# Decode attention with two mixed branches: part of one set's query weights as an indirect DMA to 48 partitions

## The chip, the cores and the metric

One Trainium2 chip, one core of it. The metric is the device time of one execution in microseconds, the median of several runs. Each core has sixteen DMA engines; a load of 128 partitions is spread over all of them, 8 partitions each.

## The reference

One token (`x`, 448 wide) goes through two attention branches with cached keys and values, and the outputs are mixed by a gate. All numbers are 32-bit floats. Branch A has 16 heads with a key and a value cache each; branch B has 16 query heads on 8 caches. Each cache is 8192 x 256.

```python
q = x @ wq                       # 16 heads of 256
scores = q . k * 256 ** -0.5     # over 8192 cached keys
o = softmax(scores) . v
branch = o.reshape(4096) @ wo    # back to 448
g = sigmoid((x * gate_w).sum())
out = g * A(x) + (1 - g) * B(x)
```

The caches are 403 MB of the 432 MB that the kernel reads.

## The kernel before

The work is cut into 8 **sets**. A set is one cache of B (unit 2, which serves two query heads) and two heads of A (units 0 and 1). Each unit has 4 **tiles** of 16 x 128 keys; a tile of keys or values is 128 partitions x 4096 columns. TILES numbers the 96 tiles.

Everything that is read lies in DRAM as one array, `stream`, in the order of use. `plan` writes this order: keys of tile i, values of tile i - 3, a set's query weights (`wq`, 3584 columns) a few tiles ahead of the set, its output weights (`wo`, 3584 columns) some tiles after it. It then cuts the order into **fills** of at most FULL = 15872 columns, 7936 KB. Pieces are cut only at multiples of their ATOM (512 columns for keys, values and `wq`, 448 for `wo`). There are 54 fills, numbered from 0; the last three are cut into smaller loads, so that the end is fed in small steps.

The main loop takes a slot of the ring (3 slots, 15936 columns) for each fill, and SP issues its load (L470). SP waits there until the slot's former fill has been read by all who use it. `piece` then emits the work of each piece:

- `project` (L222) multiplies `x` with `wq`. The weights of a set are 14 pieces of 128 rows: the 448 rows of the weights are KF = 3 blocks of 128 and a rest of 64, for the branches B (`a` = 0) and A (`a` = 1). The rests of both lie together in the last piece, one in partitions 0 to 63 and one in 64 to 127. `xz` holds `x` for each block, in column 0 of 32 columns of zeros. The query comes out in PSUM, rows 0 (B) and 32 (A) of `q`, 512 columns, and goes to SBUF (L226). `spread` turns it into the forms that the scores need.
- `scores` (L257 on PE, L263 to L269 on DVE and ACT) for units 2 and 1, `scores_by_row` (L279, L283 on DVE) for unit 0.
- `attend` (L309 on PE) multiplies probabilities with values.
- `gather`, `combine`, `column`, `project_o`, `emit_set` end a unit and a set; some of them are put off by a number of tiles with `wait`.

The first fill begins with `xg`: 4 columns of `x` and 4 of `gate_w`. `inputs` (L194 to L196) copies `x` into `xz`. Ahead of that, POOL and DVE make constants. POOL does nothing after them. At the end PE multiplies the last set with its output weights (L399), DVE copies 112 columns (L484), SP stores them (L485). The names of the tiles in the profile are `slot` (the ring), `sm` (small PSUM tiles, the query too), `o` (attention output), `Y` (final sum).

Of the kernel before, what the change touches and what calls it, by code (L numbers as in the profile page):

```python
# [7 lines left out]
F32 = mybir.dt.float32  # L8
BF16 = mybir.dt.bfloat16
AF = mybir.ActivationFunctionType  # L10
OP = mybir.AluOpType
# [3 lines left out]
P = 128  # L15
D = 448
DH = 256
SK = 8192
NCOL = SK // P
KF = D // P  # L20
KR = D - KF * P
# [3 lines left out]
NS = 8  # L25
ROWS = 16
NT = NCOL // ROWS
FULL = 15872
LEAD = 3
BLK = 32  # L30
NB = ROWS
# [3 lines left out]
WQ = (4 * KF + 2) * DH  # L35
# [4 lines left out]
TILES = [((s, r), t) for s in range(NS) for r in UNITS for t in range(NT)]  # L40


XG = 2 * (KF + 1)
SLOT = 15936
ATOM = {"xg": XG, "k": 2 * DH, "v": 2 * DH, "wq": 2 * DH, "wo": D}


def plan():

    size = {"xg": XG, "k": ROWS * DH, "v": ROWS * DH, "wq": WQ, "wo": 8 * D}  # L50
    per = len(UNITS) * NT
    n = len(TILES)
    items = []
    for i in range(n + LEAD):
        if i == 0:
            items += [("xg", 0), ("wq", 0)]
        if i < n:
            items.append(("k", i))
        if i >= LEAD:
            items.append(("v", i - LEAD))  # L60
        if i % per == 7 and i // per + 1 < NS:
            items.append(("wq", i // per + 1))
        if i % per == LEAD + 1 and i >= per:
            items.append(("wo", i // per - 1))
    loads, room = [[]], FULL
    last = [("v", n - 3), ("v", n - 2)]
    for kind, i in items[:items.index(last[0])]:
        at, left = 0, size[kind]
        while left:
            step = min(left, room) // ATOM[kind] * ATOM[kind]  # L70
            if step:
                loads[-1].append((kind, i, at, step))
            at, left, room = at + step, left - step, room - step * (kind != "xg")
            if left:
                loads.append([])
                room = FULL

    loads = [[x] for x in loads]
    x = loads[-2][0]
    loads[-2] = [x[:2], x[2:]]  # L80
    loads[-1] += [[(kind, i, 0, size[kind])] for kind, i in last]
    at, end = 0, []
    for c in LAST_CUT:
        end.append([("v", n - 1, at, c * DH)])
        at += c * DH

    for h, e, n in ((3, 0, 2), (0, 0, 2), (1, 0, 3), (2, 1, 1)):
        end.append([("wo", NS - 1, (2 * h + e) * D, n * D)])
    return loads + [end]


LOADS = plan()


@with_exitstack
def kernel(
    ctx: ExitStack,
    tc: tile.TileContext,
    stream: bass.AP,
    out: bass.AP,  # L100
):
    nc = tc.nc
# [5 lines left out]
    const = ctx.enter_context(tc.tile_pool(name="const", bufs=1))  # L108
    small = ctx.enter_context(tc.tile_pool(name="small", bufs=2))
    ps_sc = ctx.enter_context(tc.tile_pool(name="ps_sc", bufs=2, space=PSUM))  # L110
    ps_o = ctx.enter_context(tc.tile_pool(name="ps_o", bufs=3, space=PSUM))
    ps_s = ctx.enter_context(tc.tile_pool(name="ps_s", bufs=2, space=PSUM))
# [69 lines left out]

    xz = const.tile([P, KF + 2, BLK], F32, name="xz")
    nc.vector.memset(xz, 0.0)
    gate = const.tile([1, 2], F32, name="gate")

    def clear(t, n):
# [3 lines left out]
    YY = [ps_y.tile([P, D], F32, name="Y")]  # L191

    def inputs(xs):
        nc.vector.tensor_copy(xz[:, :KF, 0], xs[:, :KF])  # L194
        nc.vector.tensor_copy(xz[:KR, KF, 0:1], xs[:KR, KF:])  # L195
        nc.vector.tensor_copy(xz[KR:, KF + 1, 0:1], xs[KR:, KF:])  # L196

    def prepare(gw):
        clear(YY[0], D)
        gp = ps_s.tile([1, 1], F32, name="sm")  # L200
        for c in range(KF + 1):
            nc.tensor.matmul(gp, xz[:, c, 0:1], gw[:, c:c + 1], start=(c == 0), stop=(c == KF))
        ge = const.tile([1, 1], F32, name="ge")
        nc.scalar.activation(ge, gp, AF.Exp, scale=-1.0)
        nc.vector.tensor_scalar(ge, ge, 1.0, None, op0=OP.add)
        nc.vector.reciprocal(gate[:, 0:1], ge)
        nc.vector.tensor_scalar(gate[:, 1:2], gate[:, 0:1], -1.0, 1.0, op0=OP.mult, op1=OP.add)
# [3 lines left out]
    QR, SC, QA = {}, {}, {}  # L211

    def project(s, c0, w):

        if c0 == 0:
            QR[s] = ps_s.tile([2 * BLK, 2 * DH], F32, name="sm")
        q = QR[s]
        for j in range(w.shape[1]):
            a, c = divmod(c0 + j, KF)
            for a in (a,) if a < 2 else (0, 1):  # L220
                c = c if c0 + j < 2 * KF else KF
                nc.tensor.matmul(q[BLK * a:BLK * (a + 1), :], xz[:, c if c < KF else KF + a, :], w[:, j, :],  # L222
                                 start=(c == 0), stop=(c == KF), skip_group_check=True)
        if c0 + w.shape[1] == 2 * KF + 1:
            QR[s] = small.tile([P, NB * BLK], F32, name="px")[:2 * BLK, :2 * DH]
            nc.scalar.activation(QR[s], q, AF.Copy)  # L226

    def spread(s):

        qt = ps_s.tile([P, 2, 2, 2], F32, name="sm")  # L230
        qr = QR.pop(s)
        for h in range(2):
            for e in range(2):
                at = h * DH + e * P
                nc.tensor.matmul(qt[:, h, e, :], qr[:, at:at + P], rows4[:2 * BLK, :2], start=True, stop=True)
        for r, a, h, M in ((2, 0, 0, 2), (0, 1, 0, 1), (1, 1, 1, 1)):
            if (s, r) in BY_ROW:
                qa = ps_s.tile([P, DH], F32, name="sm")
                nc.tensor.matmul(qa, spread32, qr[:, h * DH:(h + 1) * DH], start=True, stop=True)  # L239
                QA[s, r] = small.tile([P, DH], F32, name="qa", bufs=1)  # L240
                nc.scalar.activation(QA[s, r], qa, AF.Copy, scale=-scale)
                continue
            nc.vector.tensor_scalar(QB[s % 2, r][:, :, BLK:BLK + M], qt[:, h:h + M, :, a].rearrange("p h e -> p e h"),
                                    -scale, None, op0=OP.mult)
# [155 lines left out]
                                 start=False, stop=(last and e == 1), skip_group_check=True)  # L400


    LAST, GW = {}, {}
    per = len(UNITS) * NT
    todo = []

    def wait(n, f, *args):
        todo.append([n, f, args])

    def tick():  # L410
        for t in todo:
            t[0] -= 1
        for t in [t for t in todo if t[0] <= 0]:
            todo.remove(t)
            t[1](*t[2])

    def piece(kind, i, at, view):
        n = view.shape[-1] // ATOM[kind]
        j0 = at // ATOM[kind]
        if kind == "xg":  # L420
            inputs(view[:, :KF + 1])
            GW[0] = view[:, KF + 1:]
        elif kind == "wq":
            project(i, j0, view.rearrange("p (c n) -> p c n", c=n))
            if j0 + n < 2 * KF + 1:
                pass
            elif i == 0:
                spread(0)
                prepare(GW[0])
            else:  # L430
                wait(1, spread, i)
        elif kind == "k":
            u, t = TILES[i]
            if u in BY_ROW:
                scores_by_row(u, t, 2 * j0, view.rearrange("p (j d) -> p j d", d=DH))
            else:
                scores(u, t, j0, view.rearrange("p (c n) -> p c n", c=n))
            if j0 + n < 2 * NG:
                return
            tick()  # L440
            if t == NT - 1:
                gather(u)
                wait(1, combine, u)
                wait(2, column, u)
        elif kind == "v":
            u, t = TILES[i]
            n = view.shape[-1] // DH
            attend(u, t, at // DH, n, view.rearrange("p (j d) -> p j d", d=DH))
            if at // DH + n == ROWS:
                if t == NT - 1:  # L450
                    take(u)
                    if u != TILES[-1][0]:
                        wait(1, project_o, u)
                if i >= len(TILES) - LEAD:
                    tick()
        elif kind == "wo" and i < NS - 1:
            emit_set(i, j0, view.rearrange("p (c n) -> p c n", c=n))
            if i == NS - 2 and j0 + n == 8:
                fold()
        else:  # L460
            for j in range(n):
                LAST[divmod(j0 + j, 2)] = view[:, j * D:(j + 1) * D]

    off = 0
    for fill in LOADS:
        buf = ring.tile([P, SLOT], F32, name="slot")
        c = 0
        for load in fill:
            n = sum(x[3] for x in load)
            nc.sync.dma_start(buf[:, c:c + n], stream[off:off + P * n].rearrange("(p n) -> p n", p=P))  # L470
            off += P * n
            for x in load:
                piece(*x[:3], buf[:, c:c + x[3]])
                c += x[3]
    assert not todo
    s = NS - 1
# [76 lines left out]
```

## Time and profile before

| | |
|---|---|
| median of 3 runs | 1008.62 us (1008.54 to 1008.72) |
| the profiled execution | 1009.04 us |
| its span, first to last instruction | 1007.3 us |
| granted TensorE clock, mean | 0.778 |
| PE, DVE, ACT, POOL busy | 570.1, 458.2, 92.9, 1.9 us |
| DMA | 432.51 MB, mean 429 GB/s |

A row of the table of groups names the line, the engine, the operation, what it writes and reads, how often; then busy time in us, the mean of one in ns, and the idle time of the engine just ahead of it with what ended it. In a table of windows each row has the busy time of PE, weight loads, DVE, ACT and POOL in that stretch with the number of instructions, then the granted clock, the share of time in which the sixteen DMA engines were busy, and GB/s. A row of a DMA queue has packets, megabytes and the time of its packets as a share of sixteen engines' time; a packet counts where it begins, so that in a short window the share can go over 100%. A row of the timeline has start, duration, engine, line, operation and in brackets the idle time ahead of it. A row of DMA issues ends with the time from issue to landing.

### The profile page before, as it was taken

To read this page: it belongs to the slowest core of one execution; us is meant where nothing else is said; L and a number is where in the kernel's file an instruction comes from. 1 tells how busy PE (TensorE), PEld (TensorE's weight loads), DVE (VectorE), ACT (ScalarE), POOL (GpSimd) and SP (SyncE) were. 2 spreads that over 40 slices of the span, in tenths; PEclk is the share of its full clock that TensorE was granted. 3 is DMA by queue.
4 is the path that set the end of the run, shared out by engine and by line. 5 is a ranking of instruction groups with operands and counts; after the bars stand their busy time and mean duration, and the time that the engine had idled before them with its cause. 6 is when DMAs were issued, how large, how long until landed. Compare 5 with 4: busy or idle time off the path is not lost.

```text
span 1007.3 us, 7568 instructions
## 1 busy us (share of the span) xinstructions
PE 570.1 (57%) x3154; PEld 167.1 (17%) x3154; DVE 458.2 (45%) x644; ACT 92.9 (9%) x307; POOL 1.9 (0%) x10
## 2 busy tenths in 40 slices
PE   0845835664655555646646465545565647536557
PEld 0211211121111111112111121111111112101112
DVE  1386313961248521576215841248521585216851
ACT  0100100010100110001100001100110100101010
POOL 0000000000000000000000000000000000000000
PEclk9977877778786787787777777776787867777788
DMA  9999999999999999999999999999999999999997
GB/s 404 440 439 411 442 439 437 421 437 436 439 424 436 429 439 431 437 429 440 429 434 434 436 429 429 441 437 424 430 442 439 429 424 437 439 441 429 424 422 315
DMA packets 9114, 432.51 MB, mean 429 GB/s; under 512 B 1016, under 2 KB 1144, under 8 KB 1784
## 3 DMA queue, kind: packets, MB, share of 16 engines
q1 hardware_dynamic: 9080, 432.02, 99.2%
q8 instruction: 25, 0.41, 0.1%
q14 instruction: 9, 0.07, 0.0%
HBM read 432.02 MB, written 0.00 MB: 429 GB/s over the span
## 4 chain that ended last, share of the span: by engine, by line
DMA 72%; DVE 15%; PE 11%; ACT 1%; issue 1%; another core or an unknown queue 0%; SPq 0%; ACTq 0%; DVEq 0%
DMA slot<-in_stream_dram 72%; DVE sr L283 6%; DVE slot L279 6%; PE o L309 5%; PE sc L257 4%; PE sm L222 1%; ACT px L266 0%; DVE mn L263 0%; DVE pr L296 0%; ACT pxr L292 0%; DVE pr L269 0%; ACT ew L348 0%; DVE wr L355 0%; PE sm L373 0%
## 5 line engine op out<-in xcount | busy, mean ns | idle before, releaser
L309 PE MATMUL o<-slot,pr 128*32 128x512 f32 (+1 forms) x1536 | 342.3, 740 | 224.0 <-DMA slot<-in_stream_dram 223.9
L257 PE MATMUL sc<-slot,qb 128*32 128x512 f32 x1024 | 195.2, 713 | 112.1 <-DMA slot<-in_stream_dram 111.9
L263 DVE TENSOR_REDUCE mn<-sc 128x1 f32<-128x512 f32 x64 | 44.1, 690 | 332.5 <-PE sc L257 314.2
L279 DVE TENSOR_TENSOR slot<-slot,qa 128x4096 f32<-128x4096 f32 (+7 forms) x40 | 142.6, 3565 | 42.7 <-DMA slot<-in_stream_dram 42.7
L309 PEld LDWEIGHTS o<-slot,pr 128*32 128x32 f32 (+1 forms) x1536 | 78.6, 139 | 402.9 <-DMA slot<-in_stream_dram 253.7
L283 DVE TENSOR_REDUCE sr<-slot 128x16 f32<-128x4096 f32 (+7 forms) x40 | 142.7, 3567 | 1.4
L257 PEld LDWEIGHTS sc<-slot,qb 128*32 128x32 f32 x1024 | 45.9, 129 | 226.0 <-issue 120.0
L266 ACT ACTIVATE px<-sc,st 128x512 f32<-128x512 f32 x64 | 44.0, 688 | 407.0 <-DVE st L264 395.1
L269 DVE STREAM_TRANSPOSE pr<-px 128x512 f32<-128x512 f32 x64 | 45.6, 713 | 59.6 <-ACT px L266 59.6
L222 PE MATMUL sm<-slot,xz 128*32 128x512 f32 x128 | 45.9, 695 | 37.6 <-DVE xz L195 22.8
L292 ACT ACTIVATE pxr<-sr,st 128x16 f32<-128x16 f32 x32 | 9.8, 308 | 373.0 <-DVE st L290 373.0
L373 PE MATMUL sm<-sel,ob 128*128 128x1 f32 (+1 forms) x96 | 16.7, 278 | 35.8 <-DVE ob L319 35.8
L319 DVE SCALAR_TENSOR_TENSOR ob<-o,half,ob 128x256 f32<-128x256 f32 x24 | 11.3, 473 | 45.1 <-ACT ob L318 45.0
L373 PEld LDWEIGHTS sm<-sel,ob 128*128 128x128 f32 x96 | 14.7, 217 | 59.7 <-DVE ob L319 52.1
L222 PEld LDWEIGHTS sm<-slot,xz 128*32 128x32 f32 x128 | 11.1, 126 | 66.7 <-issue 27.2
L296 DVE TENSOR_TENSOR pr<-pxr,cols 128x256 f32<-128x256 f32 x32 | 13.6, 426 | 15.9 <-ACT pxr L292 15.9
L318 ACT ACTIVATE ob<-o,half 128x256 f32<-128x256 f32 x24 | 11.3, 470 | 42.7 <-PE o L309 42.7
L362 PE MATMUL sm<-ones,wr 1*128 1x1 f32 x48 | 9.5, 265 | 9.1 <-DVE wr L355 9.1
L239 PE MATMUL sm<-px,spread 64*128 64x256 f32 x16 | 6.6, 497 | 14.1 <-DVE es L349 14.1
L382 PE MATMUL Y<-slot,ocs 128*1 128x448 f32 x112 | 14.4, 633 | 0.0
L362 PEld LDWEIGHTS sm<-ones,wr 1*128 1x128 f32 x48 | 7.7, 200 | 31.8 <-issue 29.9
L266 ACT ACTIVATION_READ_ACCUMULATOR px<-sc,st 128x1 f32 x64 | 12.3, 193 | 0.0
(73 smaller groups left out, 138.4 us busy)
## 6 DMA issues: line engine op xcount, KB each, us to landing
slot<-in_stream_dram SPq DMA_DIRECT2D x50, 7936.0 KB, 42.4
slot<-in_stream_dram SPq DMA_DIRECT2D x1, 7940.0 KB, 21.8
slot<-in_stream_dram SPq DMA_DIRECT2D x1, 4864.0 KB, 41.2
slot<-in_stream_dram SPq DMA_DIRECT2D x2, 2048.0 KB, 25.2
slot<-in_stream_dram SPq DMA_DIRECT2D x1, 3072.0 KB, 30.0
slot<-in_stream_dram SPq DMA_DIRECT2D x1, 1280.0 KB, 20.7
slot<-in_stream_dram SPq DMA_DIRECT2D x1, 1024.0 KB, 24.3
slot<-in_stream_dram SPq DMA_DIRECT2D x2, 512.0 KB, 25.5
```

What stands on the lines that cost most here:

```text
L222: nc.tensor.matmul(q[BLK * a:BLK * (a + 1), :], xz[:, c if c < KF else KF + a, :], w[:, j, :], start=(c == 0), stop=(c == KF), skip_group_ ...
L257: nc.tensor.matmul(sc[32 * g:32 * (g + 1), :], qb[:, e, at:at + 32], kt[:, j, :], start=(e == 0), stop=(e == 1), skip_group_check=True)
L263: nc.vector.tensor_reduce(mn, sc, axis=AX.X, op=OP.min)
L266: nc.scalar.activation(px, sc, AF.Exp, bias=st[:, 0, t:t + 1], scale=-1.0, accum_out=st[:, 1, t:t + 1])
L269: nc.vector.transpose(pr.rearrange("p (q r k) -> p q k r", r=BLK, k=2), px.rearrange("p (q k c) -> p q k c", c=BLK, k=2))
L279: nc.vector.tensor_tensor(kt, kt, QA[u][:, None, :].to_broadcast([P, n, DH]), op=OP.mult)
L283: nc.vector.tensor_reduce(sc[:, j0:j0 + n], kt, axis=AX.X, op=OP.add)
L296: nc.vector.tensor_tensor(pr, px[:, :, None, :].to_broadcast([P, ROWS // 2, NG * NT, 2]), cols[:, t].rearrange("p g r -> p (g r)")[:, None ...
L309: nc.tensor.matmul(O[u][w * g:w * (g + 1), :], pr[:, j // 2, :w], vt[:, j - j0:j - j0 + 2, :], start=(t == 0 and j < 2 * P // w), stop=(t ...
L362: nc.tensor.matmul(cl, WR.pop(u).rearrange("p c x m k -> p (c x m k)"), ones[:1, :], start=True, stop=True)
L373: nc.tensor.matmul(oc[:, e, :M], OB[u][:, e::2], SEL[u][:, :M], start=True, stop=True)
L382: nc.tensor.matmul(YY[0][32 * h:32 * h + 1, :], OC[s, r][:, e, m:m + 1], wt[:, j, :], start=False, stop=(s == NS - 2 and e == 1), skip_gro ...
```

## The change

Set 4's query weights of branch B, 3 blocks of 128 rows with 512 columns, are cut at column SW = 416. The first 416 columns leave the stream. They go, 384 rows in all, to a second array `side` of 128 x 3328: SIDE_ROWS names 48 partitions, each holds 8 whole rows of 416 columns, the other 80 hold zeros. The 48 partitions are those for which 8 * (p >> 6) + (p >> 2) % 8 is one of 0, 2, 4, 7, 8, 15. In `at`, each of these partitions has its own number, each other one its number plus 100000, which is out of bounds.

At fill 23 the slot's first 3328 columns are set aside for `side`, and POOL loads them with one indirect DMA, whose rows out of bounds are skipped. The fill's part of the stream has 12064 columns in place of 15872. All that comes later is cut at other places; the number of fills stays 54. The stream has 842544 columns in place of 843784.

The set's other weights (`ws`, 2336 columns: 3 blocks of 96 columns of B, 3 blocks of 512 of A, the rests) come as one piece, not cut. `project_side` takes the place of `project` for this set: 2 products of the rests, 3 of A's blocks, 3 with 96 columns, and 8 that multiply a column of `x8` with 416 columns of `side`. `x8` holds `x` in the layout of the 48 partitions; it comes in 8 more columns of `xg`. `at` is made at the start by two iotas on POOL and seven small operations on DVE.

```diff
+SIDE_SET = 4
+SIDE_FILL = 23
+SIDE_ENGINES = (0, 2, 4, 7, 8, 15)
+SIDE_ROWS = [p for p in range(P) if (8 * (p >> 6) + (p >> 2) % 8) in SIDE_ENGINES]
+SC8 = KF * P // len(SIDE_ROWS)
+SW = 416
+SREST = 2 * DH - SW
+SIDE = SC8 * SW
+XG = 2 * (KF + 1) + SC8
...
-            items.append(("wq", i // per + 1))
+            items.append(("ws" if i // per + 1 == SIDE_SET else "wq", i // per + 1))
...
-                room = FULL
+                room = FULL - SIDE * (len(loads) - 1 == SIDE_FILL)
...
     def inputs(xs):
+        nc.vector.tensor_copy(x8, xs[:, 2 * (KF + 1):])
...
+    def project_side(s, view, far):
+
+        q = ps_s.tile([2 * BLK, 2 * DH], F32, name="sm")
+        near = view[:, :KF * SREST].rearrange("p (c n) -> p c n", c=KF)
+        full = view[:, KF * SREST:].rearrange("p (c n) -> p c n", c=KF + 1)
+        for a in range(2):
+            nc.tensor.matmul(q[BLK * a:BLK * (a + 1), :], xz[:, KF + a, :], full[:, KF, :], start=True, stop=False,
+                             skip_group_check=True)
+        for c in range(KF):
+            nc.tensor.matmul(q[BLK:2 * BLK, :], xz[:, c, :], full[:, c, :], start=False, stop=(c == KF - 1),
+                             skip_group_check=True)
+            nc.tensor.matmul(q[:BLK, SW:], xz[:, c, :], near[:, c, :], start=False, stop=(c == KF - 1),
+                             skip_group_check=True)
+        for c in range(SC8):
+            nc.tensor.matmul(q[0:1, :SW], x8[:, c:c + 1], far[:, c * SW:(c + 1) * SW], start=False, stop=(c == SC8 - 1),
+                             skip_group_check=True)
+        copy_out(s, q)
...
-    for fill in LOADS:
+    for f, fill in enumerate(LOADS):
         buf = ring.tile([P, SLOT], F32, name="slot")
         c = 0
+        if f == SIDE_FILL:
+            c = SIDE
+            FAR[0] = buf[:, :c]
+            nc.gpsimd.indirect_dma_start(FAR[0], None, side, bass.IndirectOffsetOnAxis(at[:, :1], 0),
+                                         bounds_check=P - 1, oob_is_err=False)
```

On PE, at fill 23, behind the products of tile 40's values, this stood before (the line numbers are those of the kernel before; `sm` is the query, `sc` the scores of tile 44):

```order
L309 MATMUL o<-slot,pr 32x512 [waits DMAHW7_49]
L309 MATMUL o<-slot,pr 32x512 x7
L222 MATMUL sm<-slot,xz 32x512 x8
L257 MATMUL sc<-slot,qb_133 32x512 x8
L341 MATMUL sm<-gs_1604,ones 1x32 [waits DVE_49,Activation_49]
```

and this now, with the line numbers of the changed kernel (L351 is `attend`, L299 `scores`):

```order
L351 MATMUL o<-slot,pr 32x512 [waits DMAHW7_49]
L351 MATMUL o<-slot,pr 32x512 x7
L258 MATMUL sm<-slot,xz 32x512 x2
L261 MATMUL sm<-slot,xz 32x512
L263 MATMUL sm<-slot,xz 32x96
L266 MATMUL sm<-slot,x_139 1x416 [waits DMASW0_49]
L266 MATMUL sm<-slot,x_139 1x416 x7
L299 MATMUL sc<-slot,qb_133 32x512 x3
L299 MATMUL sc<-slot,qb_133 32x512 [waits DMAHW0_49]
```

(the rows of L261 and L263 come three times in turn). The eight products became sixteen, the ninth waits for the indirect DMA, and the scores of tile 44 now wait for fill 24 in the middle, since that tile's keys are cut there.

On POOL, which had nothing behind its constants, these rows end its program now:

```order
L170 IOTA px 128x128 [waits DVE_49]
L196 IOTA at 128x1
L197 IOTA at 128x1
L516 DMA slot<-in_side_dram,at 128x3328 [waits DMAHW2_49,DMAHW3_49,DMAHW1_49,DMAHW4_49,DMAHW0_49,DMAHW5_49,DVE_49,DMAHW6_49,PE_49,Pool_49]
L614 UNCONDITIONAL_BRANCH
```

The DMA waits for the former fills of this slot and for their readers; SP's load of the rest of fill 23 does not stand behind it.

More of the change, by code (lines that the diff above doesn't have):

```diff
@@ L40 @@
 TILES = [((s, r), t) for s in range(NS) for r in UNITS for t in range(NT)]
-XG = 2 * (KF + 1)
+SIDE_SET = 4
[7 more added lines that the diff above has]
+XG = 2 * (KF + 1) + SC8
 SLOT = 15936
-ATOM = {"xg": XG, "k": 2 * DH, "v": 2 * DH, "wq": 2 * DH, "wo": D}
+ATOM = {"xg": XG, "k": 2 * DH, "v": 2 * DH, "wq": 2 * DH, "wo": D, "ws": KF * SREST + (KF + 1) * 2 * DH}
 def plan():
-    size = {"xg": XG, "k": ROWS * DH, "v": ROWS * DH, "wq": WQ, "wo": 8 * D}
+    size = {"xg": XG, "k": ROWS * DH, "v": ROWS * DH, "wq": WQ, "wo": 8 * D, "ws": ATOM["ws"]}
     per = len(UNITS) * NT
@@ L99 @@
     stream: bass.AP,
+    side: bass.AP,
     out: bass.AP,
@@ L184 @@
     nc.vector.memset(xz, 0.0)
+    x8 = const.tile([P, SC8], F32, name="x8")
+    at = const.tile([P, 4], mybir.dt.int32, name="at")
+    nc.gpsimd.iota(at[:, 0:1], pattern=[[0, 1]], base=0, channel_multiplier=1)
+    nc.gpsimd.iota(at[:, 1:2], pattern=[[0, 1]], base=sum(1 << e for e in SIDE_ENGINES), channel_multiplier=0)
+    nc.vector.tensor_scalar(at[:, 2:3], at[:, 0:1], 3, 8, op0=OP.logical_shift_right, op1=OP.bitwise_and)
+    nc.vector.tensor_scalar(at[:, 3:4], at[:, 0:1], 2, 7, op0=OP.logical_shift_right, op1=OP.bitwise_and)
+    nc.vector.tensor_tensor(at[:, 2:3], at[:, 2:3], at[:, 3:4], op=OP.bitwise_or)
+    nc.vector.tensor_tensor(at[:, 1:2], at[:, 1:2], at[:, 2:3], op=OP.logical_shift_right)
+    nc.vector.tensor_scalar(at[:, 1:2], at[:, 1:2], 1, 1, op0=OP.bitwise_and, op1=OP.bitwise_xor)
+    nc.vector.tensor_scalar(at[:, 1:2], at[:, 1:2], 100000.0, None, op0=OP.mult)
+    nc.vector.tensor_tensor(at[:, 0:1], at[:, 0:1], at[:, 1:2], op=OP.add)
     gate = const.tile([1, 2], F32, name="gate")
@@ L193, in inputs @@
     def inputs(xs):
+        nc.vector.tensor_copy(x8, xs[:, 2 * (KF + 1):])
         nc.vector.tensor_copy(xz[:, :KF, 0], xs[:, :KF])
-        nc.vector.tensor_copy(xz[:KR, KF, 0:1], xs[:KR, KF:])
-        nc.vector.tensor_copy(xz[KR:, KF + 1, 0:1], xs[KR:, KF:])
+        nc.vector.tensor_copy(xz[:KR, KF, 0:1], xs[:KR, KF:KF + 1])
+        nc.vector.tensor_copy(xz[KR:, KF + 1, 0:1], xs[KR:, KF:KF + 1])
     def prepare(gw):
@@ L224, in project, with copy_out @@
         if c0 + w.shape[1] == 2 * KF + 1:
-            QR[s] = small.tile([P, NB * BLK], F32, name="px")[:2 * BLK, :2 * DH]
-            nc.scalar.activation(QR[s], q, AF.Copy)
+            copy_out(s, q)
+    def copy_out(s, q):
+        QR[s] = small.tile([P, NB * BLK], F32, name="px")[:2 * BLK, :2 * DH]
+        nc.scalar.activation(QR[s], q, AF.Copy)
+    def project_side(s, view, far):
[13 more added lines that the diff above has]
+                             skip_group_check=True)
+        copy_out(s, q)
     def spread(s):
@@ L400, in emit @@
                                  start=False, stop=(last and e == 1), skip_group_check=True)
-    LAST, GW = {}, {}
+    LAST, GW, FAR = {}, {}, {}
     per = len(UNITS) * NT
@@ L420, in piece @@
         if kind == "xg":
-            inputs(view[:, :KF + 1])
-            GW[0] = view[:, KF + 1:]
+            inputs(view)
+            GW[0] = view[:, KF + 1:2 * (KF + 1)]
+        elif kind == "ws":
+            project_side(i, view, FAR[0])
+            wait(1, spread, i)
         elif kind == "wq":
@@ L502, in wq, with apart, rows8 @@
         return _np.concatenate(full + [_np.concatenate(rest, axis=1)[:, :, None]], axis=2).reshape(NS, P, WQ)
+    def apart(w):
+        w = w.reshape(D, NS, 2 * DH)[:, SIDE_SET]
+        rest = w[:KF * P, SW:].reshape(KF, P, SREST).transpose(1, 0, 2).reshape(P, KF * SREST)
+        far = _np.zeros((P, SIDE), w.dtype)
+        far[SIDE_ROWS] = w[:KF * P, :SW].reshape(len(SIDE_ROWS), SIDE)
+        return rest, far
+    def rows8(x):
+        c = _np.zeros((P, SC8), x.dtype)
+        c[SIDE_ROWS] = x.reshape(D)[:KF * P].reshape(len(SIDE_ROWS), SC8)
+        return c
     def col(a):
@@ L532 @@
     }
-    parts["xg"] = [_np.concatenate([col(get("A_x")), col(get("gate_w"))], axis=1)]
+    parts["xg"] = [_np.concatenate([col(get("A_x")), col(get("gate_w")), rows8(get("A_x"))], axis=1)]
+    rest, far = apart(get("B_wq"))
+    parts["ws"] = {SIDE_SET: _np.concatenate([rest, parts["wq"][SIDE_SET][:, KF * 2 * DH:]], axis=1)}
     laid = {
@@ L537 @@
             for fill in LOADS for load in fill]),
+        "side": far,
     }
```

## The prediction

> **What bounds the kernel.** I read the table of slices first, then the DMA queues, the chain that ended last, and the last microseconds in windows.
>
> ```profile
> DMA  9999999999999999999999999999999999999997
> q1 hardware_dynamic: 9080, 432.02, 99.2%
> HBM read 432.02 MB, written 0.00 MB: 429 GB/s over the span
> DMA 72%; DVE 15%; PE 11%; ACT 1%; issue 1%; another core or an unknown queue 0%; SPq 0%; ACTq 0%; DVEq 0%
> 455.00:990.00 535.00, 309.62 (x1713) 90.21 (x1717) 246.00 (x338) 51.04 (x171) 0.00 (x0) 0.77 1.00 433
> ```
>
> The sixteen DMA engines are busy 99.2% of the span, while over 455 to 990 us PE works 310 of 535 us and DVE 246. The second-last column of the window row is the DMA share (1.00), the last the rate: 433 GB/s, 27.06 GB/s for one engine. The chain names DVE and PE too, because a slot's release is followed back through them, but a release comes far ahead of need:
>
> ```profile
> 833.56 0.33 SPq L470 DMA_DIRECT2D slot<-in_stream_dram  x1
> slot<-in_stream_dram SPq DMA_DIRECT2D x1, 7936.0 KB, 35.5
> ```
>
> This is the latest issue that I found, and its data lands 35.5 us later. A fill of 7936 KB takes 8.126 MB / 433 GB/s = 18.8 us, so 16.7 us of older work was still queued. The median fill is issued 42.4 us ahead. So the DMA engines never run dry, and the time is that of the engine that finishes last, plus the tail after its data. What matters now is whether all sixteen finish together:
>
> ```profile
> 996.00:998.00 2.00, 1.55 (x16) 0.55 (x14) 0.00 (x0) 0.17 (x1) 0.00 (x0) 1.00 1.01 416
> 998.00:999.00 1.00, 0.95 (x4) 0.04 (x4) 0.00 (x0) 0.00 (x0) 0.00 (x0) 1.00 0.80 323
> 998.80:999.00 0.20, 0.15 (x2) 0.00 (x0) 0.00 (x0) 0.00 (x0) 0.00 (x0) 1.00 0.64 260
> 999.00:1000.00 1.00, 0.90 (x4) 0.14 (x4) 0.00 (x0) 0.00 (x0) 0.00 (x0) 1.00 0.64 258
> 1000.00:1002.00 2.00, 0.84 (x14) 0.68 (x16) 0.48 (x1) 0.50 (x2) 0.00 (x0) 1.00 0.58 239
> 1002.80:1003.00 0.20, 0.05 (x7) 0.04 (x8) 0.00 (x0) 0.00 (x0) 0.00 (x0) 1.00 0.10 36
> ```
>
> They do not. The share falls from 1 to 0.64 between 998 and 999: 0.64 x 16 = 10.2, so six engines are done. It is 0.58 (nine) to 1002, and the last bytes go at about 1002.9. A DMA's semaphore rises by one as each engine ends its part, and the trace keeps these times. For the last load, how long before the last of sixteen each came (us):
>
> ```
> 4.93 4.84 4.76 4.69 4.47 4.26 | 3.13 | 0.63 0.59 0.58 0.57 0.51 0.48 0.46 0.26 0.00
> ```
>
> Six engines are 4.26 to 4.93 us ahead, nine end within 0.63 us. Why is seen in the packets that come from another queue:
>
> ```profile
> q8 instruction: 25, 0.41, 0.1%
> q14 instruction: 9, 0.07, 0.0%
> q1 hardware_dynamic: 8, 0.51, 195.2%
> q1 hardware_dynamic: 2, 0.13, 23.0%
> q8 instruction: 1, 0.02, 4.3%
> q1 hardware_dynamic: 4, 0.25, 154.8%
> q14 instruction: 1, 0.01, 4.8%
> ```
>
> The first two are the whole span; the third is 700 to 700.6 us, the next pair 45.4 to 46.8, the last pair 42.5 to 42.9. Share x 16 x window gives packet time: 1.952 x 9.6 / 8 = 2.342 us for a full row of 63,488 bytes. The 16 KB fetch took 0.043 x 22.4 = 0.96 us, and of the two rows starting beside it (5.15 us) one took 2.81, 0.47 longer. The 8 KB fetch took 0.31, and a row beside it 9.91 - 3 x 2.342 = 2.88, 0.54 longer. A 16 KB fetch thus costs its engine 1.43 us, and three of them make 4.29, the lead of the six. The first engines carry no fetches.
>
> **The change, part by part.**
>
> Bytes. The stream goes from 843,784 to 842,544 columns: 1,248 less of weights, 8 more beside x. Each engine serves 8 partitions, so 1,240 x 4 x 8 = 39,680 bytes less, at 27.06 GB/s **1.47 us less** on all sixteen. If the indirect DMA does what it says, six engines get 8 rows of 3,328 x 4 = 13,312 bytes, 106,496 bytes or 3.94 us: net 2.47 us more. Those with the smallest lead then end 4.26 - 2.47 = 1.79 us ahead of the old end, 0.32 ahead of the ten others, which end 1.47 ahead of it. So the ten set the end: -1.47.
>
> The price of a row from a second queue. The trace has no second data queue. Write b for what one 13 KB row costs its engine beyond its bytes. The six end at -1.79 + 8b, and decide from b = 0.04 us; at 0.22 the gain is gone. From below, rows of different fills in one queue follow one another at 433 GB/s with no loss: b = 0. From above, the 8 KB fetch, nearest in size, lost 0.31 + 0.54 - 8192 / 27.06 GB/s = 0.54 (-1.79 + 4.34 = +2.55), and the 16 KB one 1.43 - 0.61 = 0.82 (+4.8). A fetch is one lone packet into an engine's instruction store, the rows go to the same slots as the stream; so I take the value from the stream's rows, at most 0.06, which gives -1.3, and keep the other end for the range. Should an engine drain its eight rows in one visit, b is paid once: -1.79 + 0.54 or 0.82, again -1.25 to -0.97.
>
> By the Trainium skill, "DMA: Bandwidth & Descriptors", Queues, rings and completion order, an engine drains a whole packet, typically 9 to 17 descriptors, from one ring before it turns to another. By that rule the eight rows would go in one visit, at the -1.0 to -1.25 above. The trace speaks for a finer grain: the fetch at 45.5 us cut in between two stream rows, in the middle of a fill.
>
> POOL. Two iotas more at the start, beside the first load. Its DMA waits for the slot's former readers, as SP's fill 23 does (issued at 409.79); nothing is queued behind it on POOL. SP's fill 26 now also waits for the side data, whose reader PE has long finished by then.
>
> ```profile
> 409.79 0.33 SPq L470 DMA_DIRECT2D slot<-in_stream_dram  x1
> 462.01 4.57 PE L222 MATMUL sm<-slot,xz 128*32 128x512 f32 x14
> 455.62 13.93 SPq L470 DMA_DIRECT2D slot<-in_stream_dram  x2
> ```
>
> From 410 to PE's use at 462 there are 52 us. Eight rows taking turns with stream rows need 8 x (2.34 + 0.49 + 0.82) = 29 us, so PE finds them there.
>
> PE. Sixteen products take the place of eight, each two instructions in this trace. Fourteen such take 4.57 us, so eight more at full width are 5.2 us before fill 23's slot is free, which lets the second of the two issues go, at 469.2. Its data lands 42.8 us later, so 24 us are queued ahead of it: hidden. Without that cover all of it would count.
>
> ```profile
> 22.61 0.17 DVE L194 COPY xz<-slot 128x3 f32<-128x3 f32 x1 [16.59 <-DMA slot<-in_stream_dram]
> slot<-in_stream_dram SPq DMA_DIRECT2D x1, 7936.0 KB, 42.8
> q8 instruction: 1, 0.02, 3.7%
> 1002.96 1.47 PE Y L399 x32
> ```
>
> DVE. Seven small operations fall into the 16.59 us of waiting before the first load; the copy of x's rows delays PE by some 0.17 us at 22.8, under 21 us of queued fills.
>
> Shifted cuts. Behind fill 23 each fill begins up to 2,080 columns (2.5 us of stream) elsewhere, so slots come free up to that much earlier or later against the queue; 16.7 us take it. The last eight loads have the same sizes in the same order, so the tail (PE from 1002.96, then DVE and the store) keeps its length.
>
> Fetches. 25 packets of 16 KB for 6,308 PE instructions are some 256 each. The 32 further instructions pull each later fetch forward by 8 products. The 25th began at 1003.98, behind the data (the 3.7% row, window 1003.6 to 1005.2); it moves to about PE's wait at 1002.96 in old time. Should it get ahead of an engine's last rows, up to 1.43 us come back. I put 0.1 on it, within the rounding.
>
> Sum: 1009.04 - 1.3 = 1007.74 for the profiled execution. That execution stands 0.42 above the median of 1008.62, so **1007.3**.
>
> **Rivals.**
>
> 1. *Each side row pays for the turn between queues.* For it: both kinds of fetch lengthened the stream row behind them, by 0.47 and 0.54. Against it: other targets. With b = 0.54 the median is 1008.62 + 2.55 = 1011.2: slower. The point is b = 0.22, and over 0.2% from 0.48 on. At 0.82 it is 1013.4.
>
> 2. *The side rows go to engines that have no lead.* The trace names no engine; it shows six leaders, not which partitions they serve. If a set of rows falls on a late engine, or rows out of bounds still move bytes, that engine ends 2.47 behind the old end: 1011.1, slower; it decides as soon as one of the loaded engines has a lead under 2.47. If the 48 rows spread evenly, nothing changes: 1008.6. For the named set speaks only that it has six members.
> The Trainium skill, same page, Latency and other measured facts, says that engines 7 and 15 are usually the slower ones. Both are in the list; by that rule two late engines get side rows, and this rival's 1011.1 would hold. The same page ties it to software descriptor rings, which no run here has used so far.
>
> 3. *A late engine meets one more fetch, or a moved cut delays a slot.* About the old time, 1008.6.
>
> **How the numbers follow.** Forecast 0.52 (1006.9 to 1007.9). Rival 1: 0.27, of which 0.12 lies beyond +2.0 us. Rival 2: 0.13 (0.04 even; 0.09 slow, of which 0.03 for two of the six being late ones). Rival 3: 0.08. A measurement of this kernel tells about 0.2% (2.0 us) from no change; filling every engine's idle end could bring at most the mean of the leads, 2.2 us, so faster by over that has 0.02. Slower: 0.12 + 0.09 + 0.02 = 0.23. Within: 0.75. The range goes from 1006.9 to rival 1 at the 8 KB price, 1011.2; beyond it lie the 16 KB price and what the sum lacks.
>
> **What would show it.** Right: a new queue with some 48 packets and 0.64 MB, each near 0.5 us, in the 30 us behind 410; a DMA share that stays near 1 to about 1001 and then falls in one step; the last PE group at about 1001.5. If b decides, the share falls first to about 0.4 and six engines work on alone. If the rows sit on late engines, the share still drops to 0.64 or lower, and the end lies 2.5 us later. Wrong altogether would be a DMA share under 1 before 990, or PE waiting at the new products.

## The result, and the profile after

| | before | changed kernel |
|---|---|---|
| median of 22 runs each | 1008.75 us (1008.45 to 1010.21) | 1007.29 us (1006.91 to 1008.55) |
| ratio to before | | 0.9986, 95% interval 0.9979 to 0.9992 |
| the profiled execution | 1009.04 us | 1008.22 us |
| its span | 1007.3 us | 1005.5 us |

The medians differ by 1.46 us, clear of no change, and less than the 0.2% that a single measurement was held able to tell. The profiled execution of the changed kernel spends 2.7 us outside its span, that of before 1.7; the comparison rests on the medians.

From the page of the changed kernel, slices and queues:

```profile
DMA  9999999999999999999999999999999999999998
q1 hardware_dynamic: 9080, 431.39, 99.2%
q0 software_dynamic: 144, 0.64, 0.2%
q8 instruction: 24, 0.39, 0.1%
DMA slot<-in_stream_dram 71%; PE o L351 7%; PE sc L299 5%; DVE sr L325 5%; DVE slot L321 5%; PE sm L243 1%; ACT px L308 1%; PE sm L266 0%; DVE pr L311 0%; DVE mn L305 0%; PE sm L281 0%; ACT pxr L334 0%; DVE pr L338 0%; PE sm L415 0%; DVE ob L361 0%
```

The DMA engines are still what is full. The new queue moved 0.64 MB: 48 rows of 13,312 bytes, and 96 packets of 4 bytes. Sixteen of those are completions, one for each engine; the other 80 are as many as the rows out of bounds, and the kernel below without such rows has only the sixteen.

The last microseconds of the changed kernel in windows (the last two columns are DMA share and GB/s):

```profile
998.00:999.00 1.00, 0.83 (x8) 0.00 (x0) 0.00 (x0) 0.06 (x1) 0.00 (x0) 1.00 1.01 414
999.00:1000.00 1.00, 0.01 (x1) 0.02 (x1) 0.48 (x1) 0.41 (x1) 0.00 (x0) 1.00 0.97 403
1000.00:1001.00 1.00, 1.00 (x24) 0.95 (x28) 0.00 (x0) 0.17 (x1) 0.00 (x0) 1.00 0.80 315
1001.00:1002.00 1.00, 0.90 (x43) 0.63 (x36) 0.00 (x0) 0.00 (x0) 0.00 (x0) 1.00 0.12 45
```

Before, the share stood near 0.6 for the last three microseconds. Now it stays near 1 to 1000 and then falls at once. The sixteen parts of the last load, each as its time ahead of the last one (us), before and after:

```
before  4.93 4.84 4.76 4.69 4.47 4.26 3.13 0.63 0.59 0.58 0.57 0.51 0.48 0.46 0.26 0.00
after   3.40 1.12 1.10 1.09 1.08 0.97 0.86 0.83 0.79 0.76 0.75 0.68 0.67 0.58 0.26 0.00
```

Fifteen engines now end within 1.12 us. The one that was 3.13 ahead, and took no rows, still is. The mean of the leads, which is what even filling could still bring, fell from 2.2 to 0.9 us.

The packet records name no engine either. But the next packet of an engine begins within some ns of the end of the one ahead of it (3 ns before it as a rule, never more than 26), so the packets can be strung together to sixteen sequences, one for each engine. In the changed kernel, up to 990 us, six sequences carry eight side rows each and none of the 16 KB fetches. Eight others carry all 24 of these, three each, in turn. One carries five of the 8 KB fetches. One carries three of them, and it is the one far ahead. The last 8 KB fetch lies on one of the six.

The end of the chain that ended last, of before:

```profile
984.43 18.49 DMA slot<-in_stream_dram
1002.92 0.04 issue
1002.96 1.47 PE Y L399 x32
1004.46 0.28 DVE ys L484
```

and of the changed kernel:

```profile
983.08 18.47 DMA slot<-in_stream_dram
1001.55 0.04 issue
1001.59 0.99 PE Y L441 x32
1002.61 0.28 DVE ys L534
```

The landing that frees PE's last products came 1.37 us earlier. The products themselves took 0.99 in place of 1.47. That half microsecond is no part of the change: in the execution of before the granted clock stood at 0.60 in that stretch, and in the profile of every other kernel below, kernels without a gain among them, the group takes 0.99. It is about as much as the 0.42 us by which that execution stood above its median when the prediction was made.

POOL's issue, two short stretches of the queues (416.1 to 416.9 in the first two lines, 420.0 to 420.4 in the third), and PE's new products, in the changed kernel:

```profile
412.23 1.16 POOL L516 DMA_INDIRECT slot<-in_side_dram,at  x1 [408.64 <-PE o L351]
```

```profile
q1 hardware_dynamic: 3, 0.13, 36.7%
q0 software_dynamic: 3, 0.04, 11.7%
q1 hardware_dynamic: 5, 0.32, 183.0%
```

```profile
462.43 1.64 PE L258 MATMUL sm<-slot,xz 128*32 128x512 f32 x4
466.35 4.00 PE L266 MATMUL sm<-slot,x 128*1 128x416 f32 x11
```

In the first stretch three side rows begin: 0.117 x 16 x 0.8 / 3 = 0.50 us each. In the second five stream rows begin, each directly behind a side row, and 1.830 x 16 x 0.4 / 5 = 2.342 us is what each takes. In the packet records all 48 side rows take 498 ns (their bytes at 27.06 GB/s are 492), and each of the 40 full stream rows behind one takes 2342 ns, as without. They come one by one, on each of the six engines a side row every 2.83 us; the first of all begins at 416.9 us, the last at 437.1. PE's first side product at 465 has no wait ahead of it.

### The profile page after: what moved, and what is told of

Its sections match the earlier page's. It is cut to its first block, busy times and chain, and to the rows that moved or that the text cites. A ratio compares the mean times of both kernels' runs of the same rounds, so it can differ in the third digit from the quotient of the medians.

```text
span 1005.5 us, 7618 instructions
## 1 busy us (share of the span) xinstructions
PE 586.8 (58%) x3170; PEld 173.1 (17%) x3170; DVE 458.7 (46%) x650; ACT 93.0 (9%) x307; POOL 3.2 (0%) x13
## 4 chain that ended last, share of the span: by engine, by line
DMA 71%; PE 14%; DVE 13%; ACT 1%; issue 1%; SPq 0%; ACTq 0%; DVEq 0%
DMA slot<-in_stream_dram 71%; PE o L351 7%; PE sc L299 5%; DVE sr L325 5%; DVE slot L321 5%; PE sm L243 1%; ACT px L308 1%; PE sm L266 0%; DVE pr L311 0%; DVE mn L305 0%; PE sm L281 0%; ACT pxr L334 0%; DVE pr L338 0%; PE sm L415 0%; DVE ob L361 0%
## 5 line engine op out<-in xcount | busy, mean ns | idle before, releaser
L351 PE MATMUL o<-slot,pr 128*32 128x512 f32 (+1 forms) x1536 | 345.2, 759 | 201.7 <-DMA slot<-in_stream_dram 201.7
L299 PE MATMUL sc<-slot,qb 128*32 128x512 f32 x1024 | 196.5, 726 | 111.5 <-DMA slot<-in_stream_dram 111.3
L321 DVE TENSOR_TENSOR slot<-slot,qa 128x4096 f32<-128x4096 f32 (+6 forms) x39 | 142.4, 3651 | 42.9 <-DMA slot<-in_stream_dram 42.9
L351 PEld LDWEIGHTS o<-slot,pr 128*32 128x32 f32 (+1 forms) x1536 | 80.4, 142 | 378.6 <-DMA slot<-in_stream_dram 224.9
L325 DVE TENSOR_REDUCE sr<-slot 128x16 f32<-128x4096 f32 (+6 forms) x39 | 142.5, 3654 | 1.3
L299 PEld LDWEIGHTS sc<-slot,qb 128*32 128x32 f32 x1024 | 46.3, 130 | 229.1 <-issue 128.5
L243 PE MATMUL sm<-slot,xz 128*32 128x512 f32 x112 | 41.1, 717 | 36.0 <-DVE xz L216 22.9
L415 PE MATMUL sm<-sel,ob 128*128 128x1 f32 (+1 forms) x96 | 17.9, 290 | 32.9 <-DVE ob L361 32.9
```

The costliest lines, as they stand in the source:

```text
L299: nc.tensor.matmul(sc[32 * g:32 * (g + 1), :], qb[:, e, at:at + 32], kt[:, j, :], start=(e == 0), stop=(e == 1), skip_group_check=True)
L321: nc.vector.tensor_tensor(kt, kt, QA[u][:, None, :].to_broadcast([P, n, DH]), op=OP.mult)
L325: nc.vector.tensor_reduce(sc[:, j0:j0 + n], kt, axis=AX.X, op=OP.add)
L351: nc.tensor.matmul(O[u][w * g:w * (g + 1), :], pr[:, j // 2, :w], vt[:, j - j0:j - j0 + 2, :], start=(t == 0 and j < 2 * P // w), stop=(t ...
L415: nc.tensor.matmul(oc[:, e, :M], OB[u][:, e::2], SEL[u][:, :M], start=True, stop=True)
```

## The experiments

All times below are medians, from 8 to 11 runs of each kernel; the kernel before, run beside them on the same chip, had 1008.53 us in the first four and 1008.52 in the last three. The changed kernel's 1007.29 was taken beside a kernel before of 1008.75, so a comparison with it is uncertain by these 0.2 us. The diffs are against the changed kernel.

**Rows on other engines.**

```diff
-SIDE_ENGINES = (0, 2, 4, 7, 8, 15)
+SIDE_ENGINES = (1, 3, 5, 6, 9, 10)
```

> The side rows go to the partitions of engines 1, 3, 5, 6, 9, 10 in place of 0, 2, 4, 7, 8, 15; cuts, bytes and work stay those of the changed kernel. Theory (the gain is 1.47 us of bytes off the engines that end last, and the six named ones have a lead of 4.3 us that takes the rows): some loaded engine has no lead and ends 2.47 us behind the old end less its lead of 0 to 0.6, so +1.9 to +2.5 us on the kernel before: 1010.6 to 1011.3, ratio 1.0019 to 1.0025; at the end the DMA share falls to about 0.4 or lower while a few engines work on. Rival (the gain comes from the moved cuts, the smaller stream or a shorter tail on PE, whichever engines take the rows): 1007.3 as in the changed kernel.

Measured: 1010.77 us (1010.32 to 1011.79), ratio 1.0022, interval 1.0013 to 1.0031. Its last microseconds:

```profile
997.00:998.00 1.00, 1.00 (x14) 0.18 (x2) 0.00 (x0) 0.00 (x0) 0.00 (x0) 1.00 0.65 267
1000.00:1001.00 1.00, 0.81 (x6) 0.10 (x4) 0.00 (x0) 0.00 (x0) 0.00 (x0) 1.00 0.64 259
1002.00:1003.00 1.00, 0.00 (x0) 0.00 (x0) 0.43 (x1) 0.47 (x1) 0.00 (x0) 1.00 0.38 156
1003.00:1004.00 1.00, 0.90 (x20) 0.85 (x21) 0.05 (x1) 0.17 (x1) 0.00 (x0) 1.00 0.32 134
```

Six engines are idle from 997 on, four more from about 1002, and five or six end alone. The last load's leads are 7.5 to 8.4 for six engines, 3.5 to 3.9 for four, 2.5 for one, and 0 to 0.2 for five: five late engines and the one in between took the rows. In the packet sequences these are four engines with 16 KB fetches, the one with five 8 KB fetches and the one with three. Same cuts, same bytes, same work, and 2.24 us slower in place of 1.46 faster: which engines take the rows decides, and the formula with p >> 6 and p >> 2 names them rightly for this indirect DMA.

**Rows on all sixteen.**

```diff
-SIDE_ENGINES = (0, 2, 4, 7, 8, 15)
+SIDE_ENGINES = tuple(range(16))
```

> The same weights come as an indirect DMA to all 128 partitions, 3 rows each, none out of bounds; each engine moves the bytes that it moved before. Theory: no engine is relieved, so 0 +- 0.3 us: 1008.4 to 1009.1, with the six engines 4 us ahead at the end as before. Rival (the second queue or the piece's new form brings the gain by itself): 1007.3.

Measured: 1008.57 us (1008.46 to 1009.72), ratio 1.0001, interval 0.9992 to 1.0010. Its windows:

```profile
998.00:999.00 1.00, 1.00 (x12) 0.35 (x8) 0.00 (x0) 0.00 (x0) 0.00 (x0) 0.89 0.82 328
999.00:1000.00 1.00, 0.95 (x8) 0.04 (x4) 0.00 (x0) 0.00 (x0) 0.00 (x0) 1.00 0.63 255
1001.00:1002.00 1.00, 0.90 (x20) 0.85 (x21) 0.05 (x1) 0.17 (x1) 0.00 (x0) 1.00 0.56 235
```

The second queue and the new form of the weights change nothing by themselves; the six engines lie idle for the last 4 us as before.

**Without the side load.** This kernel computes set 4's query from other columns.

```diff
-            FAR[0] = buf[:, :c]
-            nc.gpsimd.indirect_dma_start(FAR[0], None, side, bass.IndirectOffsetOnAxis(at[:, :1], 0),
-                                         bounds_check=P - 1, oob_is_err=False)
+            FAR[0] = buf[:, c + 4096:2 * c + 4096]
```

> The indirect DMA is left out; the eight products read other columns of the slot, so the query of set 4 is computed from wrong weights. Cuts and stream are those of the changed kernel. Theory (side rows lie wholly in the lead of the six): the ten others set the end as in the changed kernel, 1007.3, ratio 0.9985; the six end 4.3 us or so ahead of the last again, plus the tail's spread. Rival (the rows or their queue cost the end something): faster than the changed kernel by that, up to 0.9 us, the mean lead that is left there.

Measured: 1007.24 us (1006.80 to 1008.55), ratio 0.9988, interval 0.9979 to 0.9997. Its windows:

```profile
997.00:998.00 1.00, 1.00 (x11) 0.14 (x4) 0.00 (x0) 0.00 (x0) 0.00 (x0) 1.00 0.64 260
1000.00:1001.00 1.00, 0.86 (x34) 0.56 (x31) 0.00 (x0) 0.17 (x1) 0.00 (x0) 1.00 0.50 197
1001.00:1002.00 1.00, 0.94 (x32) 0.63 (x32) 0.00 (x0) 0.00 (x0) 0.00 (x0) 1.00 0.02 7
```

Without the rows the time is that of the changed kernel, and the six engines again stop 4 us early (leads 3.8 to 4.6). So the rows cost nothing that can be measured.

**The side load twice.**

```diff
+            for _ in range(2):
                 nc.gpsimd.indirect_dma_start(FAR[0], None, side, bass.IndirectOffsetOnAxis(at[:, :1], 0),
                                              bounds_check=P - 1, oob_is_err=False)
```

> The same indirect DMA twice, the second behind the first: 8 more rows of 0.498 us on the same six engines. Theory (the lead is 4.3 us, of which the change uses up all but 0.3): the six end 2.2 us behind the old end, 1010.3 to 1011.2, ratio 1.0015 to 1.0024, and at the end the DMA share stays near 6/16 = 0.38 for about 3 us. Rival (there is more room in the six than the lead says, or rows from the second queue lie beside the stream's): 1007.3.

Measured: 1010.88 us (1010.75 to 1011.52), ratio 1.0024, interval 1.0015 to 1.0034. Its windows:

```profile
1000.00:1001.00 1.00, 0.99 (x4) 0.14 (x4) 0.00 (x0) 0.00 (x0) 0.00 (x0) 1.00 0.92 371
1001.00:1002.00 1.00, 0.80 (x6) 0.14 (x4) 0.00 (x0) 0.00 (x0) 0.00 (x0) 1.00 0.55 220
1002.00:1003.00 1.00, 0.31 (x2) 0.00 (x0) 0.08 (x1) 0.47 (x1) 0.00 (x0) 1.00 0.39 160
1003.00:1004.00 1.00, 0.54 (x4) 0.54 (x4) 0.41 (x1) 0.00 (x0) 0.00 (x0) 1.00 0.39 161
```

Now the share goes to 0.39 of sixteen: the six work on alone, the others are done. Eight more rows are 3.98 us of one engine; 3.6 of them show against the changed kernel's 1007.29, 3.8 if each is set against the kernel before beside it, and 3.49 in the last landing of the two profiled executions. The room in the six was thus some 0.2 to 0.5 us; the leads of the kernel before had said 0.32.

**More fetches of PE's program.**

```diff
         pr = PR[u, t]
+        for j in range(11 if j0 + n == ROWS else 0):
+            nc.tensor.matmul(YY[0][:1, :4], zero[:, :1], zero[:, :4], start=False, stop=False, skip_group_check=True)
```

> The changed kernel with 11 tiny products of zeros added to each of 96 tiles, 2112 PE instructions more, 8.25 packets of 16 KB. Theory (the leads come from PE's fetches, 1.43 us each, on the engines without a lead): eight engines get one more, so +1.4 us on the changed kernel: 1008.4 to 1009.0, and the first six are again 1.4 us or so ahead of the last; 32 or 33 fetches in the record. Rival (the leads have another cause, and PE has room for 1056 short products): 1007.3.

Measured: 1008.95 us (1008.25 to 1010.22), ratio 1.0005, interval 0.9996 to 1.0014. Queues of its page, and a window:

```profile
q0 software_dynamic: 144, 0.64, 0.2%
q8 instruction: 33, 0.54, 0.2%
```

```profile
1001.00:1002.00 1.00, 0.79 (x16) 0.78 (x20) 0.15 (x1) 0.12 (x1) 0.00 (x0) 1.00 0.51 211
```

Nine fetches more inside the span than the changed kernel's 24, and 1.66 us on its median. In the packet sequences up to 990 us each of eight engines now has four of them in place of three. The six with side rows and the one with five 8 KB fetches are 1.6 to 2.4 us ahead of the last again at the last load, the eight all within 0.7. The interval does not tell this kernel from the kernel before, but it lies wholly above that of the changed kernel (0.9979 to 0.9992), and the leads moved as the theory says: the lead is made by fetches on other engines.

**A wider side.**

```diff
-SW = 416
+SW = 448
```

> 448 columns in place of 416 on the side. Theory: the ten lose another 0.11 us, the six carry 0.30 us of rows more and 0.11 of stream less, and their lead in front of the ten falls from 0.32 to about 0: 1007.2, 0.1 us under the changed kernel, too little to be told apart. Rival (side rows cost more than their bytes): 1007.5 or more.

Measured: 1007.20 us (1006.85 to 1008.04), ratio 0.9988, interval 0.9979 to 0.9997: where it was expected, and not to be told from the changed kernel. Its fifteen engines end within 1.02 us.

**The same bytes in eight loads.**

```diff
-            nc.gpsimd.indirect_dma_start(FAR[0], None, side, bass.IndirectOffsetOnAxis(at[:, :1], 0),
-                                         bounds_check=P - 1, oob_is_err=False)
+            for h in range(SC8):
+                nc.gpsimd.indirect_dma_start(FAR[0][:, h * SW:(h + 1) * SW], None, side,
+                                             bass.IndirectOffsetOnAxis(at8[:, h:h + 1], 0),
+                                             bounds_check=SC8 * P - 1, oob_is_err=False)
```

(`side` is laid out as eight blocks of 128 rows, and `at8` holds eight columns of row numbers.)

> The side data in eight indirect DMAs of 416 columns, 64 rows of 1664 bytes for each engine in place of 8 of 13312, the same bytes. Theory (a loaded engine takes one row from the second queue for each row of the stream): 64 turns of 2.4 us, so the data is not there at 462 us but only when the stream's queue has run dry at about 494 us; PE waits some 30 us for it, the slot comes free late and the stream stands still for 7 to 13 us: 1014 to 1021. Rival (an engine takes many rows in a visit): the data is there in time, 1007.3 to 1008.

Measured: 1008.77 us (1008.11 to 1009.67), ratio 1.0001, interval 0.9991 to 1.0011. Both expectations missed. Its queue on the page, a wait between 460 and 500 us, SP's issue of fill 26 in the timeline, and that issue with its size and time to landing:

```profile
q0 software_dynamic: 512, 0.64, 0.2%
```

```profile
PE sm L269 <- DMA slot<-in_side_dram,at: 12.9, 2, 8.3
```

```profile
486.04 0.33 SPq L525 DMA_DIRECT2D slot<-in_stream_dram  x1
```

```profile
slot<-in_stream_dram SPq DMA_DIRECT2D x1, 7936.0 KB, 22.5
```

In the packet records a loaded engine has four packets for each of the eight loads: 4992, 4992 and 3328 bytes (three rows, three and two) and 4 bytes that complete the load. Nearly all of them come one at a time between two stream rows. A loaded engine so had some 32 turns, 24 of them for data, not 64 and not 8; the last data packet began at 479.8 us, the last completion at 482.2. PE waited for them twice, 4.6 and 8.3 us, until 482.73. The slot of fill 23 came free late, and fill 26 was issued at 486.04 and landed 22.5 us later, of which 18.8 are its own: the queue ahead of it was nearly empty. In the packet records the six engines that came to its end first stand still for 3.5 us in sum between 485.6 and 487.2, and their first rows of fill 26, begun at 487.0 to 487.2 us, take 0.6 to 1.3 us longer than 2.34. That is 8.8 us together, or 0.55 for each of sixteen. The kind of loss was the expected one, its size not, since the data came much sooner than 64 turns would bring it.

The median is 1.48 us over the changed kernel's, and the last landing of the profiled execution 1.14 us. Load by load, the engines of this kernel are on the mean 0.2 us behind those of the changed kernel at fill 25 and 0.7 to 0.9 behind from fill 26 to the end of the large fills. The engines that lost time there were ahead, so how much of the loss reaches the end depends on where the later fetches fall; that it makes the whole 1.48 was not shown.

## Why the prediction was right, point by point

**The bound.** That the time is that of the last DMA engine was right. The same bytes on other engines gave +2.24 us, on all sixteen nothing, on the six early ones -1.46.

**The lead of the six, and its cause.** The 4.26 us came back as 3.8 to 4.6 in the kernel without side load, and the second side load found 0.2 to 0.5 us of room where 0.32 was left by the estimate. That the early engines are free of fetches rested on the price of 1.43 us for each 16 KB alone: three times this is the lead. The packet sequences show it. In the kernel before, up to 470 us, the six sequences that are furthest ahead have no fetch at all, and the 16 KB fetches lie in turn on eight others; in the changed kernel the six with side rows have none of these. One more on each of the eight then cost 1.66 us and put the six ahead once more. Two details the prediction lacked: the ninth late engine carries no 16 KB fetch but five of 8 KB, at 0.84 us each or about 4.2 in all, and the engine that is 3.13 ahead carries three of 8 KB, at 0.55 us each.

**Bytes.** -1.47 was forecast for the ten others. The landing that PE's end waits for moved by 1.37 us, the medians by 1.46.

**The price of a row from a second queue.** This was the widest unknown: 0, or 0.54 to 0.82 from the fetches. It is 6 ns a row, and nothing on the row behind it. The value taken, from the stream's own rows, was the right end. The 0.17 us set aside for it (1.47 less 1.3) were not needed. That the forecast still met the median within 0.01 us is luck: the sum by the term of bytes alone gives 1007.15 from the median shown then, 1007.28 from the one over 22 runs.

**How the queues take turns.** By the Trainium skill, "DMA: Bandwidth & Descriptors", Queues, rings and completion order, a visit takes a whole packet of typically 9 to 17 descriptors. Here a side row of 13,312 bytes was a packet by itself and the turns went row by row, one side row every 2.83 us; with rows of 1664 bytes three stood in a packet of 4992. A turn cost next to nothing either way (a packet of 4992 bytes took 192 ns, by its bytes 184), so the changed kernel's time does not depend on it; that of the eight small loads does, since it sets when the data is there.

**Side rows on late engines** (the second rival) did not happen with the set as written; when it was made to happen it gave 1010.77, against a price of 1011.1. The Trainium skill's rule that engines 7 and 15 are usually slower (same page, Latency and other measured facts) is not seen here: the six engines that the set names, 7 and 15 among them by its formula, were the earliest before, and with all six loaded all but one of the sixteen end within 1.12 us.

**POOL, PE, cuts.** POOL issued at 412.23, the last side row ended at 437.6 and the last completion came at 439.3, PE asked at 465. The sixteen products ran from 462.4 to 470.7, where the eight had run to 467.4, 3.3 us for the 5.2 allowed. Fill 26 went out at 471.62 in place of 469.2 and landed 36.7 us later, so 17.9 us of older work still covered it. No moved cut delayed a slot: the DMA share is 1.00 from 455 to 990 and 0.99 from there to 1000.

**Fetches at the end.** This small step was wrong. The 25th fetch was to move forward, to PE's wait near the end. The four ahead of it did, by 5 to 15 us, but it moved back: the page has 24 inside the span, and in the packet records the 25th begins at 1007.2 us, 1.7 us after the span's end. Why is not settled; the 0.1 us put on it is too small to see.

## What to carry to other kernels

When the DMA engines are full throughout, look at how far apart they end: the share in windows of the last microseconds, and the sixteen parts of the last landing. An engine that also carries program fetches loses time there that no total shows, and moving bytes from late to early engines gains what is taken off the late ones, up to the mean of the leads; the same bytes on the wrong engines lose more than that. In these runs rows from a second queue cost their bytes alone, but they arrived one packet for each row of the stream, and a load's completion took a turn too, so what is cut small must be started long before it is needed.

## What the runs showed of the hardware

- A row out of bounds of an indirect DMA is no row skipped altogether: 80 such rows left 80 packets of 4 bytes, 9 ns each, eight on each of the ten other engines.
- The eight rows of 1664 bytes that one small load brings to an engine were put together to packets of 4992, 4992 and 3328 bytes; rows of 13,312 and 63,488 bytes stand alone.
- A 16 KB fetch of PE's program costs its DMA engine 1.43 us, 2.4 times its bytes, and the fetches go in turn over eight of the sixteen engines; a 13 KB row from a second data queue costs 0.498 us, its bytes.
